# Making the second half of the first expert block's input during the last attention unit

## The chip, the cores and the metric

The kernel runs on one core of a Trainium2 chip. The metric is device time in microseconds (us), of one launch. PE is TensorE (matmuls), DVE is VectorE, ACT is ScalarE, POOL is GpSimd, and SP is SyncE, which here only issues DMA transfers.

## The reference

Attention with a learned relative-position bias, for 4 batches, 8 heads, 576 positions and head dimension 64, in float32; then a feed-forward layer over the 2304 tokens, with d_model 512 and d_ff 2048:

```
scores = q @ k.T / 8 + bias[h, i, j]
attn   = exp(scores - max) / (sum + 1e-9)
x      = (attn @ v), heads side by side        # 2304 x 512
h      = x @ w_in                              # 2304 x 2048
g      = h if h >= 1, 0 if h <= -1, else (h + 1)^2 / 4
out    = g @ w_out                             # 2304 x 512
```

All matmuls reach float32 accuracy by splitting an operand into a high part (rounded to the type that PE multiplies) and a low part (what rounding took away), and adding two or three products.

## The kernel before

**Three stages.** First the bias table is made (up to about 100 us, line 186 on). Then come 16 attention units, one for each pair of heads `p` and batch `b`, numbered `n = 4 p + b` (line 644). Each has five steps `k`: `scores` (line 493) multiplies queries and keys, DVE adds the bias and takes the maximum, ACT does the exponential; `transposes`, `shared` and `split` (lines 563, 581, 545) turn the result and split it into high and low parts; `values` (line 603) multiplies by the values, once for each half of the positions, and writes the product transposed to the DRAM buffers `xT`. `recips` (line 591) writes the reciprocal row sums to `rT`. A unit's transposes and values lag behind its scores, so the last unit's `values` end well after its scores. Last comes the feed-forward stage (line 713): three blocks of 768 tokens, each in two halves `j` of 384 tokens. For each of 16 slices `f` of d_ff and each half, `up_proj` (line 725) does 12 matmuls of 384 columns, `act` (line 735) makes g and its two parts, and `down_proj` (line 746) does 9 matmuls of 512 columns, some half-slices later (`finish`, line 766).

**The input x.** `split_x` (line 431) makes one quarter of a half: head pair `k` (128 rows of d_model) by 384 tokens. It loads two products from `xT` and the reciprocals from `rT`, broadcast over 64 partitions. DMAs are issued by SP: two for `xT`, and two for each piece into which the reciprocals fall (one piece for the first half of block 0, three for its second half, which crosses two batches). Then it adds the two products (line 457 or 460), multiplies (458 or 461), casts to the high part on ACT (462), and subtracts for the low part (464 or 466). With `early` the three others run on POOL, without it on DVE.

**Where block 0's x is made.** The table `xt` gives, for the four quarters of the first half, the unit and step at which the load and the arithmetic are written (lines 698 to 702): units 14 and 15, all through one raw tile in `m_raw`. The second half is written at the start of the feed-forward stage (line 781 on), on DVE, with three raw tiles in turn (`ring`, lines 99 and 723), two of them in `m_raw2`, which lies where the attention's bias tiles were. Its high and low parts lie in `m_x1`, also in room that the attention gives back.

**Weights.** `weight` (line 105) loads the raw float64 weights, and ACT (lines 114, 115, 118), DVE (116) and POOL (119) turn them into a high and a low part. Slices 0 and 1 are made in unit 15 (`wt`), through one raw tile; slice f + 2 is written behind `up_proj` of slice f, with raw tiles in `m_raw` and `m_raw2`.

**The order of work.** Each engine takes its instructions in a fixed order, and an instruction that waits holds those behind it. That order is set when the program is built, by a planner that takes instructions by their place in the program text and by its own estimate of when their operands and tiles are free; it may move work ahead or back within these limits. Instructions passed to `pool` keep their written order up to unit 14 (`go`). SP's DMAs are one such order, too.

**Rooms.** A tile with a tag lies in one of the tag's buffers and waits until the tile that had it is done. Units 14 and 15 are the last to use the key tiles (`kh`, `kl`), the value tiles (`vs`) and the raw tiles (`qk`, `v`).

Of the kernel before, what the change touches and what calls it, by code (L numbers as in the profile page):

```python
# [8 lines left out]
F32 = mybir.dt.float32  # L9
F32R = mybir.dt.float32r  # L10
# [3 lines left out]
ALU = mybir.AluOpType  # L14
# [16 lines left out]
CB = sum(CBW)  # L31
CFG = dict(ex=(9, 2, 0, 2, 9), bb=5, mv=1, hi='pvvpv', rb='a', lag=(1, 1), dr=(3, 1, 2, 2, 2), pool=((0, 1), (2, 0), (2, 1), (3, 0), (3, 1)), sb=4, keep=1, drain=2, diag='a', rb2='v', eps='v', rc=2, rbb=1, hb=2, rawb=(2, 2), t=(3, 10, 7, 10, 16, 11, 12, 18), eb=4, seq=0, yl=(2, 4, 12, 15, 16, 18, 20, 22, 24, 28, 30), yr=(3, 8, 19, 23, 35), ns=(1,) * NG, fw=2, pb=(6, 9, 12, 14, 16), pq=22, tb=6, ub=12, w1=('p', 'p', 'p', 'p'), wcp=('v', 'a', 'a', 'v'), wl=('p', 'v', 'p', 'p'), ms='ppvp', low0='ppp', anch=(8, 8, 16, 23, 23), low1='ppp', ob=6, gb=3, fin=2, xt=((14, 0), (14, 1), (14, 2), (14, 4), (14, 4), (15, 0), (15, 1), (15, 3)), wt=((15, 1), (15, 4)), lastp=15, ch=(0, 24, 52, 84, 112, 144), sbf=('v', 'v', 'v', 'v', 'v'), bsE=(), ytail='p')
EPS = 1e-9
RB = 2
LASTP = CFG["lastp"]
XT = CFG["xt"]
# [12 lines left out]
@with_exitstack  # L49
def attn_cpb_moe_kernel(ctx, tc, qk, vL, cb, win, wout, lw, dd, ident, ii, out):  # L50
    nc = tc.nc
# [6 lines left out]
    TH = TB // 2  # L58
# [40 lines left out]
    ring = [(rps[0], 1)]  # L99

    def x_pool():
        turn[1] += 1
        return ring[turn[1] % len(ring)]
# [30 lines left out]
    def pool(ins):  # L134
        if KEEP and go[0]:
            tc.keep_in_program_order(ins)
# [49 lines left out]
    with ExitStack() as ph:  # L186
# [24 lines left out]
        diag = [ac.tile([P, P], F32, name=f"diag{i}") for i in range(2)]  # L211
# [6 lines left out]
        pq = cp.tile([P, 2, C, H], F32, name="pq")  # L218
# [176 lines left out]
        for G in range(NG):  # L395
# [6 lines left out]
            i, g = G // 5 + 1, G % 5  # L402
# [28 lines left out]
    def split_x(blk, k, j, early=False):  # L431

        src = xT[k][blk // TB][:, :, TH * j : TH * j + TH].rearrange("(s d) i c -> d s i c", s=2)
        rp, n_ = x_pool()
        r = rp.tile([P, 3, TH], F32, tag="x", name=f"x{blk}_{k}_{j}", bufs=n_)
        for i in range(2):
            nc.sync.dma_start(out=r[D * i : D * i + D, 0:2], in_=src[:, :, i])
        c0 = blk + TH * j
        c1 = c0
        while c1 < c0 + TH:  # L440
            t = c1 % S
            e = min(c0 + TH, c1 - t + (512 if t < 512 else S))
            for i in range(2):
                at = 512 * i + t if t < 512 else 1024 + D * i + t - 512
                row = rT[k][c1 // S][at : at + e - c1].unsqueeze(0)
                nc.sync.dma_start(out=r[D * i : D * i + D, 2, c1 - c0 : e - c0], in_=row.to_broadcast((D, e - c1)))  # L446
            c1 = e

        z = (2 * (blk // TB) + j) % 3
        h = xps[z].tile([P, TH], F32R, tag=f"xh{k}", name=f"xh{blk}_{k}_{j}")  # L450
        l = xps[z].tile([P, TH], F32R, tag=f"xl{k}", name=f"xl{blk}_{k}_{j}")
        xs[blk, k, j] = h, l
        x = r[:, 0]

        def parts():
            if early:
                early[0](nc.gpsimd.tensor_tensor(out=x, in0=x, in1=r[:, 1], op=ALU.add))
                early[0](nc.gpsimd.tensor_tensor(out=x, in0=x, in1=r[:, 2], op=ALU.mult))
            else:
                nc.vector.tensor_tensor(out=x, in0=x, in1=r[:, 1], op=ALU.add)  # L460
                nc.vector.tensor_tensor(out=x, in0=x, in1=r[:, 2], op=ALU.mult)
            nc.scalar.copy(h, x)
            if early:
                early[0](nc.gpsimd.tensor_tensor(out=l, in0=x, in1=h.bitcast(F32), op=ALU.subtract))  # L464
            else:
                nc.vector.tensor_tensor(out=l, in0=x, in1=h.bitcast(F32), op=ALU.subtract)  # L466

        if early:
            return parts
        parts()  # L470

    with ExitStack() as ph:
# [154 lines left out]
        xlo = {}  # L627

        def drain(keep, mid=None, at=0):
            while len(queue) > keep:  # L630
# [6 lines left out]
        def step(i_):  # L637
            for m in range(3):
                for t, i in STEPS:
                    if t == 20 - 10 * m + i_ and 0 < n + m < N:  # L640
                        preps[n + m][i]()

        go[0] = True
        for n in range(N):
            p, b = n // B, n % B
            if n + 2 < N:
                preps[n + 2] = prep(n + 2)
            es[n] = []
            if n >= LASTP:
                go[0] = False  # L650
            for k in range(5):
                e, later = scores(n, k, qkv[n], bias[p])
                es[n].append(e)
                exps = [False]

                def exp_():
                    if not exps[0]:
                        exps[0] = True
                        for f in later:
                            exps.append(f())  # L660

                if CFG["ex"][k] == 0:
                    exp_()
                step(2 * k)
                if b == B - 1 and p + 1 < NP:
                    bias.setdefault(p + 1, []).append(load_bias(p + 1, k))

                def tr(n=n, k=k):
                    half = k // 2 if k < 4 else 1
                    if k in (0, 2):  # L670
                        w = 256 + D * half
                        eT[n, half] = (
                            (tp0, tp1)[half].tile([P, 9, w], F32R, tag=f"hi{half}", name=f"hi{n}_{half}"),
                            (tp0, tp1)[half].tile([P, 9, w], F32R, tag=f"lo{half}", name=f"lo{n}_{half}"),
                        )
                    transposes(n, k, es[n], eT[n, half])
                    if k in (1, 4):
                        shared(n, half, es[n], eT[n, half])

                def rc(n=n):  # L680
                    recips(n)

                if k in (1, 4):
                    def av(n=n, half=0 if k == 1 else 1):
                        values(n, half, es[n], eT[n, half], qkv[n]["v"])
                    queue.append([tr, rc] if k == 4 else [tr])
                    late.append([CFG["lag"][0 if k == 1 else 1], [av]])
# [25 lines left out]
    with ExitStack() as ph:  # L713
# [162 lines left out]
```

## Time and profile before

| what | value |
|---|---|
| median of 3 runs | 815.49 us (813.03 to 820.22) |
| profiled execution | 815.15 us, of which the span of the trace is 813.4 us |
| PE busy, share of the span | 90% |
| DVE, ACT, POOL busy | 61%, 57%, 51% |
| mean granted clock of PE | 0.96 |
| 40 slices of the span, PE busy in tenths, slices 18 to 22 | 9, 7, 5, 9, 9 |

The span is cut into 40 slices of 20.3 us. The chain of waits names, backwards from the end, what released each instruction. A wait of an engine is shown as the idle time ahead of an instruction and what ended it.

### The profile page before, as it was taken

Reading aid. Unit: us, or ns where it says so; the run is one execution under the profiler, and the core shown is the slowest. Engines: PE = TensorE matmul, PEld = TensorE weight load, DVE = VectorE, ACT = ScalarE, POOL = GpSimd, SP = SyncE. Lnnn points to the kernel's source line nnn. Section 1 sums busy time; section 2 is a strip of 40 time slices with the busy share of each in tenths; the row PEclk is TensorE's granted clock in tenths of the full one; section 3 lists DMA queues with packets and bytes.
Section 4 is the critical chain, followed back from the end, with each engine's and each line's share of the span. In section 5 each row is a group of like instructions: output and inputs, shape, how many; then the busy total and the mean of one; then the engine's idle time right before and its main releaser. Section 6 shows DMA issues by size and latency. Waiting matters only on the chain. (4 is left out here: it accounts for less than half of the span.)

```text
span 813.4 us, 13433 instructions
## 1 busy us (share of the span) xinstructions
PE 732.9 (90%) x4692; PEld 645.8 (79%) x4692; DVE 499.6 (61%) x1021; ACT 467.2 (57%) x1014; POOL 418.3 (51%) x385
## 2 busy tenths in 40 slices
PE   2766789899989999987599989999999999999998
PEld 1232579898989989986489888999999999999996
DVE  8999868788768888866475566276322243222222
ACT  1986668788878888877398854343222233222222
POOL 5774767788766878874177744222222222222221
PEclk9967999999999999998889999999999999999999
DMA  6667787876786687435566454054000012000002
GB/s 195 181 193 207 205 197 209 234 196 176 186 247 165 165 238 175 115 106 169 178 210 206 145 176 114 1 158 134 20 1 1 1 30 77 1 1 1 1 0 79
DMA packets 58660, 103.60 MB, mean 127 GB/s; under 512 B 12496, under 2 KB 32608, under 8 KB 58592
## 3 DMA queue, kind: packets, MB, share of 16 engines
q1 hardware_dynamic: 44976, 83.08, 35.5%
q0 software_dynamic: 2304, 9.96, 6.0%
q10 hardware_dynamic: 11312, 9.70, 3.9%
q8 instruction: 37, 0.61, 0.3%
q14 instruction: 31, 0.25, 0.1%
HBM read 67.63 MB, written 25.12 MB: 114 GB/s over the span
## 5 line engine op out<-in xcount | busy, mean ns | idle before, releaser
L743 POOL TENSOR_TENSOR gl<-c,gh 128x384 fp32r<-128x384 f32 x96 | 101.9, 1061 | 247.5 <-ACT gh L742 225.0
L740 ACT ACTIVATE c<-c,half_s 128x384 f32<-128x384 f32 x96 | 59.1, 615 | 169.0 <-DVE c L739 169.0
L730 PE MATMUL h<-xh,wi 128*128 128x384 f32 x384 | 132.6, 345 | 12.3 <-DVE c L741 6.4
L739 DVE TENSOR_SCALAR c<-h 128x384 f32<-128x384 f32 x96 | 53.3, 555 | 147.2 <-PE h L732 144.2
L731 PE MATMUL h<-xl,wi 128*128 128x384 f32 x384 | 131.4, 342 | 1.0 <-POOL xl L464 0.7
L732 PE MATMUL h<-xh,wi 128*128 128x384 f32 x384 | 131.4, 342 | 0.7 <-POOL wi L119 0.7
L557 POOL TENSOR_TENSOR lo<-c,hi 128x512 fp32r<-128x512 f32 x75 | 101.9, 1363 | 58.4 <-DVE hi L556 55.9
L753 PE MATMUL y<-wo,gl 128*128 128x512 f32 x288 | 114.2, 396 | 0.0
L752 PE MATMUL y<-wo,gh 128*128 128x512 f32 x288 | 113.9, 396 | 0.0
L751 PE MATMUL y<-wo,gh 128*128 128x512 f32 x288 | 112.6, 391 | 0.0
L510 DVE CUSTOM_DVE_ANT_0 e<-S,bias 128x576 f32<-128x576 f32 x128 | 93.8, 745 | 21.1 <-PE S L508 19.9
L517 ACT ACTIVATE e<-e,mx 128x576 f32<-128x576 f32 x128 | 99.7, 780 | 4.5 <-DMA v<-in_vL_dram 1.9
L507 PE MATMUL S<-kh,qa 128*128 128x288 f32 x256 | 79.5, 326 | 18.5 <-DMA kh<-kh 6.9
L730 PEld LDWEIGHTS h<-xh,wi 128*128 128x128 f32 x384 | 73.5, 191 | 20.8 <-DVE c L741 9.9
L741 DVE TENSOR_TENSOR c<-h,c 128x384 f32<-128x384 f32 x96 | 53.3, 556 | 50.3 <-ACT c L740 50.3
L742 ACT CAST gh<-c 128x384 fp32r<-128x384 f32 x96 | 49.2, 512 | 51.2 <-DVE c L741 50.1
L731 PEld LDWEIGHTS h<-xl,wi 128*128 128x128 f32 x384 | 73.5, 191 | 6.0 <-DVE xl L466 1.3
L572 PE MATMUL T<-id_s,e 128*128 128x128 f32 x512 | 74.1, 278 | 2.6 <-ACT e L517 1.5
L732 PEld LDWEIGHTS h<-xh,wi 128*128 128x128 f32 x384 | 73.5, 191 | 1.1 <-POOL wi L119 1.1
L508 PE MATMUL S<-ls,qa 128*128 128x288 f32 x256 | 72.3, 300 | 0.0
L507 PEld LDWEIGHTS S<-kh,qa 128*128 128x128 f32 x256 | 48.6, 190 | 26.4 <-DVE mx L510 11.8
L572 PEld LDWEIGHTS T<-id_s,e 128*128 128x128 f32 x512 | 61.6, 143 | 4.3 <-ACT e L517 1.9
(141 smaller groups left out, 1557.5 us busy)
## 6 DMA issues: line engine op xcount, KB each, us to landing
bias_d<-y SPq DMA_DIRECT2D x36, 295.5 KB, 3.3
qk<-in_qk_dram SPq DMA_DIRECT2D x16, 608.0 KB
qa<-in_qk_dram POOLq DMA_DIRECT2D x16, 608.0 KB, 6.6
x<-xT SPq DMA_DIRECT2D x48, 192.0 KB, 3.4
rawi<-in_win_dram SPq DMA_DIRECT2D x16, 512.0 KB, 4.6
rawo<-in_wout_dram SPq DMA_DIRECT2D x16, 512.0 KB, 3.7
v<-in_vL_dram SPq DMA_DIRECT2D x16, 320.0 KB, 3.4
qa<-ls SPq DMA_DIRECT2D x32, 152.0 KB, 3.4
```

Source lines behind the costliest of these rows:

```text
L507: nc.tensor.matmul(ps[:, hf, :HS], qs[:, qc], kh[:, kc : kc + HS], start=True, stop=False)
L510: nc.vector.tensor_tensor_reduce(out=ev.rearrange("p (a b) -> p a b", a=2), in0=ps[:, :, :HS], in1=bias[k][:, S * j : S * j + S].rearrange ...
L517: lambda ev=ev, j=j: nc.scalar.activation(ev, ev, AF.Exp, bias=mx[:, j : j + 1], scale=-1.0, accum_out=sm[:, 4 * j + k : 4 * j + k + 1])
L557: r = nc.gpsimd.tensor_tensor(out=lo, in0=m, in1=hi.bitcast(F32), op=ALU.subtract)
L572: nc.tensor.transpose(ps[:, tb, :], e[:, c0 : c0 + P], id_s)
L730: nc.tensor.matmul(ps[:, :TH], wh_, xh, start=k == 0, stop=False)
L731: nc.tensor.matmul(ps[:, :TH], wh_, xl, start=False, stop=False)
L732: nc.tensor.matmul(ps[:, :TH], wl_, xh, start=False, stop=k == NK - 1)
L743: nc.gpsimd.tensor_tensor(out=gl, in0=c, in1=gh.bitcast(F32), op=ALU.subtract)
L751: nc.tensor.matmul(y, gh[:, c], wo[f][0], start=f == 0, stop=False)
L752: nc.tensor.matmul(y, gh[:, c], wo[f][1], start=False, stop=False)
L753: nc.tensor.matmul(y, gl[:, c], wo[f][0], start=False, stop=f == NF - 1)
```

## The change

The table `xt` becomes `xa`: for each half `j` and each quarter, the step at which its load is written, the step of its arithmetic, the room of its raw data, and the engine (`p` POOL, `v` DVE). The second half of block 0 is now written in unit 15, two quarters on POOL and two on DVE. Three of its raw quarters lie in a buffer of the tags `kh`, `kl` and `vs`, the fourth in the one raw tile in `m_raw`. The last quarter of the first half moves to a buffer of the bias tag and is written some steps earlier. The high and low parts of the second half lie in the attention's raw tiles: three to a `qk` buffer, one to a `v` buffer (`x_tile`); `a_load` stays open to the end for that, and `m_x1` goes. In the later blocks the three raw tiles of x are one of `m_raw`, one of `m_x2` (which had two), and the room of the raw weights in `m_raw`. The arithmetic on x, the number of DMAs and their sizes stay as they are.

```
-CFG = dict(... xt=((14, 0), (14, 1), (14, 2), (14, 4), (14, 4), (15, 0), (15, 1), (15, 3)) ...)
+CFG = dict(xa=((((14, 0), (14, 1), '', 'p'), ((14, 2), (14, 4), '', 'p'),
+                ((14, 4), (15, 0), '', 'p'), ((14, 3), (15, 1), 'bias', 'p')),
+               (((15, 0), (15, 1), 'kh', 'p'), ((15, 0), (15, 2), 'kl', 'v'),
+                ((15, 1), (15, 3), 'vs', 'p'), ((15, 1), (15, 4), '', 'v'))) ...)
...
+    lp = ctx.enter_context(tc.tile_pool(name="a_load", side="right", bufs=2))
     bp = loads.enter_context(tc.tile_pool(name="a_bias", side="right", bufs=CFG["bb"]))
-    lp = loads.enter_context(tc.tile_pool(name="a_load", side="right", bufs=2))
...
+    def x_tile(z, k, part, name):
+        if z != 1:
+            return xps[z].tile([P, TH], F32R, tag=f"x{'hl'[part]}{k}", name=name)
+        at = 2 * k + part
+        g = min(at // 3, 2) + (at == 7)
+        if at % 3 == 0 or at == 7:
+            tag, w, n_ = ("qk", QW, CFG["rawb"][0]) if g < 2 else ("v", 10 * D, CFG["rawb"][1])
+            room[g] = lp.tile([P, w], F32R, tag=tag, name=name, bufs=n_)
+        c0 = TH * (at % 3 if at < 6 else 0)
+        return room[g][:, c0 : c0 + TH]
...
-            if early:
-                early[0](nc.gpsimd.tensor_tensor(out=x, in0=x, in1=r[:, 1], op=ALU.add))
-                early[0](nc.gpsimd.tensor_tensor(out=x, in0=x, in1=r[:, 2], op=ALU.mult))
+            if early == "p":
+                pool(nc.gpsimd.tensor_tensor(out=x, in0=x, in1=r[:, 1], op=ALU.add))
+                pool(nc.gpsimd.tensor_tensor(out=x, in0=x, in1=rr, op=ALU.mult))
             else:
                 nc.vector.tensor_tensor(out=x, in0=x, in1=r[:, 1], op=ALU.add)
...
-                    if (n, k) == XT[2 * i]:
-                        xlo[i] = split_x(0, i, 0, [pool])
-                    if (n, k) == XT[2 * i + 1]:
-                        xlo[i]()
+                    for j in range(2):
+                        ask, make, home, e = XA[j][i]
+                        if (n, k) == ask:
+                            r = None
+                            if home:
+                                po, w, n_ = dict(kh=(qp, QW, CFG["hb"]), kl=(qp, QW, 2), vs=(qp, 10 * P, 2), bias=(bp, 2 * S, CFG["bb"]))[home]
+                                r = po.tile([P, w], F32, tag=home, name=f"rx{j}_{i}", bufs=n_)
+                                r = r[:, : 3 * TH].rearrange("p (a b) -> p a b", a=3)
+                            xe[i, j] = split_x(0, i, j, e, r)
+                        if (n, k) == make:
+                            xe[i, j]()
...
-        xps.append(ph.enter_context(tc.tile_pool(name="m_x1", bufs=1)))
+        xps.append(None)
...
-            ring[1:] = [(xp, 2)] * 2
+            ring[1:] = [(xp, 1), (rps[0], 0)]
```

## Rows read from the trace of the kernel before

**Rows 1.** Busy time by stretch: length, PE, PEld, DVE, ACT, POOL (instructions), granted clock, DMA, GB/s.
```profile
370.00:388.60 18.60, 15.77 (x78) 13.77 (x77) 11.27 (x18) 13.69 (x33) 7.57 (x6) 0.74 0.67 194
388.60:413.00 24.40, 14.51 (x51) 11.28 (x51) 12.29 (x19) 12.15 (x22) 7.60 (x6) 0.78 0.62 190
413.00:470.00 57.00, 54.59 (x271) 48.28 (x270) 35.44 (x49) 48.37 (x88) 42.94 (x33) 1.00 0.56 181
```

**Rows 2.** Waits of PE from 412 us to the end: total, times, longest.
```profile
PE h L730 <- DVE c L741: 2.6, 2, 2.4
```

**Rows 3.** PE in order of time: start, length, line, [idle before, what ended it].
```profile
388.59 0.52 PE L730 MATMUL h<-xh,wi 128*128 128x384 f32 x1
...
391.12 0.44 PE L730 MATMUL h<-xh,wi 128*128 128x384 f32 x1 [1.57 <-DVE c L741]
...
403.81 0.69 PE L730 MATMUL h<-xh,wi 128*128 128x384 f32 x1 [3.95 <-ACT xh L462]
...
408.71 0.52 PE L730 MATMUL h<-xh,wi 128*128 128x384 f32 x1
...
412.98 0.38 PE L730 MATMUL h<-xh,wi 128*128 128x384 f32 x1
...
416.44 0.34 PE L730 MATMUL h<-xh,wi 128*128 128x384 f32 x1
...
418.55 0.39 PE L751 MATMUL y<-wo,gh 128*128 128x512 f32 x1
...
420.63 0.33 PE L730 MATMUL h<-xh,wi 128*128 128x384 f32 x1
```

**Rows 4.** SP's DMA issues in order of time: start, length, line, count.
```profile
395.48 1.25 SPq L437 DMA_DIRECT2D x<-xT  x2
396.77 3.80 SPq L446 DMA_DIRECT2D x<-rT  x6
400.62 0.58 SPq L109 DMA_DIRECT2D rawi<-in_win_dram  x1
```

**Rows 5.** PE instructions from 388.5 to 412.9 us, lines 730, 751, 752.
```profile
388.50:412.90 24.40, 6.30 (x13) 0.78 0.62 190
388.50:412.90 24.40, 1.81 (x4) 0.78 0.62 190
388.50:412.90 24.40, 1.18 (x3) 0.78 0.62 190
```

**Rows 6.** DVE in order of time around the attention's end.
```profile
388.83 0.56 DVE L739 TENSOR_SCALAR c<-h 128x384 f32<-128x384 f32 x1 [1.29 <-PE O L614]
...
390.50 0.56 DVE L741 TENSOR_TENSOR c<-h,c 128x384 f32<-128x384 f32 x1 [1.11 <-ACT c L740]
```

**Rows 7.** PE, then POOL, in order of time: what frees the rooms.
```profile
348.12 0.29 PE L529 MATMUL S_L<-ls,qa 128*128 128x288 f32 x1
...
365.12 0.31 PE L614 MATMUL O<-lo,vs 128*128 128x320 f32 x1
...
367.25 1.02 POOL L464 TENSOR_TENSOR xl<-x,xh 128x384 fp32r<-128x384 f32 x1 [0.62 <-ACT xh L462]
```

**Rows 8.** ACT's group of casts to x's high part, 340 to 410 us: busy, mean ns, idle before.
```profile
L462 ACT CAST xh<-x 128x384 fp32r<-128x384 f32 x8 | 4.1, 510 | 14.2 <-DVE x L461 9.2 <-POOL x L458 5.1
```

**Rows 9.** POOL, then DVE, in order of time: x's arithmetic side by side and alone.
```profile
378.04 1.12 POOL L464 TENSOR_TENSOR xl<-x,xh 128x384 fp32r<-128x384 f32 x1 [2.68 <-ACT xh L462]
...
378.22 1.35 DVE L460 TENSOR_TENSOR x<-x 128x384 f32<-128x384 f32 x1
...
395.18 0.55 DVE L460 TENSOR_TENSOR x<-x 128x384 f32<-128x384 f32 x1
```

**Rows 10.** POOL in order of time: the last step of slice 2's first weight.
```profile
407.88 1.28 POOL L119 TENSOR_TENSOR wi<-ai,wi 128x512 fp32r<-128x512 f32 x1 [13.04 <-ACT wi L118]
```

**Rows 11.** The page's DMA issues: count, KB each, median us to landing.
```profile
x<-xT SPq DMA_DIRECT2D x48, 192.0 KB, 3.4
```

**Rows 12.** POOL in order of time: the last step of slice 15's second weight.
```profile
498.99 1.62 POOL L119 TENSOR_TENSOR wo<-ao,wo 128x512 fp32r<-128x512 f32 x1
```

More of the change, by code (lines that the diff above doesn't have):

```diff
@@ L31 @@
 CB = sum(CBW)
-CFG = dict(ex=(9, 2, 0, 2, 9), bb=5, mv=1, hi='pvvpv', rb='a', lag=(1, 1), dr=(3, 1, 2, 2, 2), pool=((0, 1), (2, 0), (2, 1), (3, 0), (3, 1)), sb=4, keep=1, drain=2, diag='a', rb2='v', eps='v', rc=2, rbb=1, hb=2, rawb=(2, 2), t=(3, 10, 7, 10, 16, 11, 12, 18), eb=4, seq=0, yl=(2, 4, 12, 15, 16, 18, 20, 22, 24, 28, 30), yr=(3, 8, 19, 23, 35), ns=(1,) * NG, fw=2, pb=(6, 9, 12, 14, 16), pq=22, tb=6, ub=12, w1=('p', 'p', 'p', 'p'), wcp=('v', 'a', 'a', 'v'), wl=('p', 'v', 'p', 'p'), ms='ppvp', low0='ppp', anch=(8, 8, 16, 23, 23), low1='ppp', ob=6, gb=3, fin=2, xt=((14, 0), (14, 1), (14, 2), (14, 4), (14, 4), (15, 0), (15, 1), (15, 3)), wt=((15, 1), (15, 4)), lastp=15, ch=(0, 24, 52, 84, 112, 144), sbf=('v', 'v', 'v', 'v', 'v'), bsE=(), ytail='p')
+CFG = dict(xa=((((14, 0), (14, 1), '', 'p'), ((14, 2), (14, 4), '', 'p'), ((14, 4), (15, 0), '', 'p'), ((14, 3), (15, 1), 'bias', 'p')), (((15, 0), (15, 1), 'kh', 'p'), ((15, 0), (15, 2), 'kl', 'v'), ((15, 1), (15, 3), 'vs', 'p'), ((15, 1), (15, 4), '', 'v'))), ex=(9, 2, 0, 2, 9), bb=5, mv=1, hi='pvvpv', rb='a', lag=(1, 1), dr=(3, 1, 2, 2, 2), pool=((0, 1), (2, 0), (2, 1), (3, 0), (3, 1)), sb=4, keep=1, drain=2, diag='a', rb2='v', eps='v', rc=2, rbb=1, hb=2, rawb=(2, 2), t=(3, 10, 7, 10, 16, 11, 12, 18), eb=4, seq=0, yl=(2, 4, 12, 15, 16, 18, 20, 22, 24, 28, 30), yr=(3, 8, 19, 23, 35), ns=(1,) * NG, fw=2, pb=(6, 9, 12, 14, 16), pq=22, tb=6, ub=12, w1=('p', 'p', 'p', 'p'), wcp=('v', 'a', 'a', 'v'), wl=('p', 'v', 'p', 'p'), ms='ppvp', low0='ppp', anch=(8, 8, 16, 23, 23), low1='ppp', ob=6, gb=3, fin=2, wt=((15, 1), (15, 4)), lastp=15, ch=(0, 24, 52, 84, 112, 144), sbf=('v', 'v', 'v', 'v', 'v'), bsE=(), ytail='p')
 EPS = 1e-9
@@ L35 @@
 LASTP = CFG["lastp"]
-XT = CFG["xt"]
+XA = CFG["xa"]
 NX = [((14, 0), (14, 1), (14, 1), (15, 0)), ((4, 0), (6, 0), (8, 0), (10, 0))]
@@ L429, in attn_cpb_moe_kernel, with split_x @@
     xs = {}
-    def split_x(blk, k, j, early=False):
-        src = xT[k][blk // TB][:, :, TH * j : TH * j + TH].rearrange("(s d) i c -> d s i c", s=2)
-        rp, n_ = x_pool()
-        r = rp.tile([P, 3, TH], F32, tag="x", name=f"x{blk}_{k}_{j}", bufs=n_)
+    room = {}
+    def x_tile(z, k, part, name):
[8 more added lines that the diff above has]
+        return room[g][:, c0 : c0 + TH]
+    def split_x(blk, k, j, early=False, raw=None):
+        src = xT[k][blk // TB][:, :, TH * j : TH * j + TH].rearrange("(s d) i c -> d s i c", s=2)
+        if raw is None:
+            rp, n_ = x_pool()
+            if n_:
+                r = rp.tile([P, 3, TH], F32, tag="x", name=f"x{blk}_{k}_{j}", bufs=n_)
+                r, rr = r[:, 0:2], r[:, 2]
+            else:
+                r = rp.tile([P, 2 * DM], F32, tag="raw", name=f"x{blk}_{k}_{j}")[:, : 2 * TH].rearrange("p (a b) -> p a b", a=2)
+                rr = rp.tile([P, DM], F32, tag="a", name=f"xr{blk}_{k}_{j}")[:, :TH]
+        else:
+            r, rr = raw[:, 0:2], raw[:, 2]
         for i in range(2):
-            nc.sync.dma_start(out=r[D * i : D * i + D, 0:2], in_=src[:, :, i])
+            nc.sync.dma_start(out=r[D * i : D * i + D], in_=src[:, :, i])
         c0 = blk + TH * j
@@ L445, in split_x @@
                 row = rT[k][c1 // S][at : at + e - c1].unsqueeze(0)
-                nc.sync.dma_start(out=r[D * i : D * i + D, 2, c1 - c0 : e - c0], in_=row.to_broadcast((D, e - c1)))
+                nc.sync.dma_start(out=rr[D * i : D * i + D, c1 - c0 : e - c0], in_=row.to_broadcast((D, e - c1)))
             c1 = e
         z = (2 * (blk // TB) + j) % 3
-        h = xps[z].tile([P, TH], F32R, tag=f"xh{k}", name=f"xh{blk}_{k}_{j}")
-        l = xps[z].tile([P, TH], F32R, tag=f"xl{k}", name=f"xl{blk}_{k}_{j}")
+        h = x_tile(z, k, 0, f"xh{blk}_{k}_{j}")
+        l = x_tile(z, k, 1, f"xl{blk}_{k}_{j}")
         xs[blk, k, j] = h, l
@@ L455, in parts @@
         def parts():
-            if early:
-                early[0](nc.gpsimd.tensor_tensor(out=x, in0=x, in1=r[:, 1], op=ALU.add))
-                early[0](nc.gpsimd.tensor_tensor(out=x, in0=x, in1=r[:, 2], op=ALU.mult))
+            if early == "p":
+                pool(nc.gpsimd.tensor_tensor(out=x, in0=x, in1=r[:, 1], op=ALU.add))
+                pool(nc.gpsimd.tensor_tensor(out=x, in0=x, in1=rr, op=ALU.mult))
             else:
                 nc.vector.tensor_tensor(out=x, in0=x, in1=r[:, 1], op=ALU.add)
-                nc.vector.tensor_tensor(out=x, in0=x, in1=r[:, 2], op=ALU.mult)
+                nc.vector.tensor_tensor(out=x, in0=x, in1=rr, op=ALU.mult)
             nc.scalar.copy(h, x)
-            if early:
-                early[0](nc.gpsimd.tensor_tensor(out=l, in0=x, in1=h.bitcast(F32), op=ALU.subtract))
+            if early == "p":
+                pool(nc.gpsimd.tensor_tensor(out=l, in0=x, in1=h.bitcast(F32), op=ALU.subtract))
             else:
@@ L626, in attn_cpb_moe_kernel @@
         queue, late = [], []
-        xlo = {}
+        xe = {}
         def drain(keep, mid=None, at=0):
```

## The prediction

> **What bounds the kernel now.** I began with the page's slices: PE is nearly full except where the attention hands over to the feed-forward stage. The busy times by stretch put numbers on it [rows 1]: from 413 us PE is busy at full clock, but in the 24.4 us from 388.6 it is busy for 14.5 us at a mean clock of 0.78. The list of PE's waits from 412 us to the end has 2.6 us in it [rows 2]; so whatever work PE has done by 413 us fixes the end, and time won before that point is won at the end.
>
> PE's order of time shows the handover [rows 3]. At 388.59 the attention's last value matmuls are over and the first matmul of slice 0's second half (up 0,1) begins. Then PE waits: for the activation of (0,0), and again and again for the high part of a second-half quarter, up to 3.95 us at once. After that wait it runs at half clock (1.2 GHz, by the mean of 0.78): a matmul of line 730 takes 0.52 us at 408.71 where one at 416.44 takes 0.34. Behind the missing x stands SP [rows 4]: one second-half quarter takes 1.25 + 3.80 = 5.05 us of issuing (8 DMAs), about the distance at which the quarters arrive, and slice 2's first weight is issued only behind the last of them, at 400.62.
>
> **What the hole costs.** From 388.59 to 412.98 is 24.39 us [rows 3]. In it PE does 13 matmuls of line 730, as many of 731 and 732 (39 of 384 columns), and 4 + 3 + 3 = 10 of 512 columns (751 to 753; the last has as many as 752) [rows 5]. At the full rate, pipelined, twelve 384s take 418.55 - 416.44 = 2.11 us (0.176 each) and nine 512s 420.63 - 418.55 = 2.08 (0.231 each) [rows 3]. So 39 x 0.176 + 10 x 0.231 = 9.2 us of work took 24.4.
>
> **What the change removes.** With the second half ready before the attention ends, the 12 matmuls of (0,1) lie before 388.6. What stays is the activation of (0,0): it waits for the attention's last matmul, and its second half ends at 390.50 + 0.56 [rows 6], after which PE restarts at 391.12 as it does now. From there 27 x 0.176 + 10 x 0.231 = 7.1 us reach the point of 412.98, at 398.2. The gain before costs is 412.98 - 398.2 = **14.8 us**. A lower clock at the restart would cost 0.52 - 0.34 = 0.18 us a matmul, 2.2 us for a dozen; today PE restarts at 391.12 with 0.44, a first matmul at full clock, after the same value matmuls, so I take 0.
>
> **Is x ready in time?** The rooms decide. The key tiles are free when unit 14's scores are done, at 348.4; the value tile after 365.12 + 0.31, and the shared raw tile after 367.25 + 1.02 = 368.27 [rows 7]. SP needs 4 x 5.05 = 20.2 us for the 32 DMAs that move. Two quarters fit before 365.4; the third takes to 370.5, the fourth to 375.5, landing 3.4 us later [rows 11], and the chain add, multiply, cast, subtract of 4 x 0.55 ends near 381. That is 7 us before 388.6. The raw loads of slices 0 and 1 on the same queue move back by up to 5 us; slice 1's first weight then still comes about when PE restarts, so 0, with that cover thin.
>
> **What it adds.** *ScalarE.* Four casts of 0.51 us [rows 8]; one of them lies before 388.6 today, so 3 x 0.51 = 1.5 us more. ACT is busy 13.7 of 18.6 us there [rows 1] and its exponentials, casts and copies feed the last transposes, so I charge all of it: **+1.5**. *Waits in front of them.* ACT has three waits for POOL's multiply, 5.1 us together [rows 8], 1.7 each, and behind such a cast stand the attention's own casts. Two new quarters are on POOL: 2 x 1.7 = **+3.4**. For the two on DVE the bounds are 0 and 1.7 each (the row's 9.2 us for DVE all lies behind 388.6); I take 0, since the nearest one, the DVE quarter already made before 388.6, has no wait. *POOL*: 6 operations of about 1.0 us [rows 9] in 11 us of idle time [rows 1], 0. *VectorE*: 6 operations of 0.55 us come, but about as many that stand before 388.6 today go to POOL, 0. *TensorE*: 9 more matmuls before 388.6, 1.6 us at full rate, against 18.60 - 15.77 = 2.8 us of idle time [rows 1]: 0, at most 2.9 at half clock.
>
> *Weights.* Slice 2's first weight takes from 400.62 to 409.16, 8.5 us [rows 4, 10], and is wanted when PE has done (1,0), (1,1) and ten of the 512s, about 7 us after its restart. It must be issued near 389. Its raw room lies over the bias tiles, free before that, and SP is idle by then, so 0. *Later blocks.* The third raw tile becomes the weights' own, free when slice 15 is done, about 500.6 us [rows 12]. At 412.98 PE begins on slice 2, and a slice takes 2 x (2.11 + 2.08) = 8.4 us, so slice 15 comes 13 x 8.4 later, at 522, or 512 with the gain, and block 1 one slice behind: over 15 us for two quarters through that room, so 0. The single wait of 2.4 us in [rows 2] may go or move: 2.4 either way.
>
> **Sum.** 14.8 - 1.5 - 3.4 = 9.9 us less. The profiled execution took 815.15 us (0.34 below the median of 815.49): 815.15 - 9.9 = **805.2 us**.
>
> **A rule that speaks against it.** A DVE add of 0.55 us took 1.35 while POOL's subtract ran from 378.04 to 379.16 [rows 9]. The change puts x on both engines at once. The Trainium skill, SBUF — State Buffer, section "Who interferes with whom", says that a DVE instruction with two SBUF inputs contends with a GpSimd instruction that reads SBUF, and that the loser fully blocks; by that rule the trace agrees, for the DVE add ends just after POOL's operation.
>
> **Rivals.**
> (a) *Both engines block each other.* Six DVE operations at 0.80 us more each are 4.8 us, in front of the attention's evictions in DVE's order: 805.2 + 4.8 = 810.0. For it: the 1.35. Against: DVE has 18.60 - 11.27 = 7.3 us idle there [rows 1], and its attention work reads PSUM. Chance 0.10. This is the case of the rule above.
> (b) *Weights take the place of x.* If slice 2's weight still ended at 409.16, its matmuls would come not near 412 but at 409.2, and eight more 512s (1.8 us) would be done ahead: about 5 us won, 810. For it: one raw tile, ACT busy 48.4 of 57 us after 413 [rows 1]. Against: SP's queue is what held it. Chance 0.12.
> (c) *The second half comes no earlier in effect*: the planner leaves its loads behind others, and the hole stays: 813 to 817, taken as 815. For it: SP must fit 20 us more of issuing into unit 15. Chance 0.10.
> (d) *Slower: the attention's end is held up.* ACT takes its order strictly; if each of the four casts stands in front of attention work and waits as casts do behind 388.6 today (9.2 us in three waits, 3.1 each, and up to 5.05 where SP paces them), then 4 x 5.05 = 20.2, less the 14.8 won and plus 1.5 for the casts: 815.15 + 6.9 = 822. It is slower once the mean wait passes (14.8 - 1.5) / 4 = 3.3 us. Against: the rooms above open early enough. Chance 0.08.
>
> **The numbers.** My forecast has 0.60, with 800.4 (the gain of 14.8 in full) to about 809 as its own range: DVE's casts waiting as POOL's do cost 3.4 more. The range over all takes in (a) and (b) and reaches to 813, where the costs together (1.5 + 6.8 + 4.8) leave 1.7 us: that leaves out (d), most of (c), and a little below. About 1% (8 us, below 807.3 or above 823.6 by the median) is what a measurement here can tell from no change. Faster by over 1%: 0.60, nearly all of the forecast and little else. Slower by over 1%: the worse part of (d), 0.07. Same: the rest, 0.33.
>
> **What would show it.** After the change, the 12 matmuls of (0,1) should stand before the attention's last value matmul, and PE's waits for the high part of x should be gone behind it. The attention's end should move from 388.6 to about 393 (1.5 + 3.4), with waits of ACT's cast for POOL in front; if it moves by over 13, (d) holds. A wait of line 732 for POOL's line 119 behind it, or of line 730 for ACT's line 118, is (b). DVE's x operations at over 1 us are (a). SP issuing second-half quarters behind 388 is (c), and would make the prediction wrong; so would a new PE wait near 500 to 530, where the raw tile of the weights is shared.

## The result

The changed kernel took 807.56 us (median of 4 runs, 805.41 to 808.29), the kernel before 815.12 beside it (4 runs, 813.03 to 820.22): a ratio of 0.9894, 95% interval [0.9844, 0.9944]. Run once more with more runs it had 0.9865 [0.9832, 0.9897]. The forecast was 805.2 us, 0.988 of the median before. So the kernel became about 1% faster, as forecast. The terms of the sum came out differently, though, and the mechanism is told below.

**Busy time by stretch after** (columns as in [rows 1]; the profiled execution took 806.87 us, its span is 805.1):

```profile
370.00:391.00 21.00, 17.78 (x114) 16.37 (x113) 11.86 (x25) 14.64 (x36) 9.17 (x9) 0.92 0.53 150
391.00:405.00 14.00, 8.98 (x25) 6.07 (x26) 8.20 (x11) 11.81 (x22) 7.50 (x6) 0.76 0.83 273
405.00:470.00 65.00, 63.06 (x320) 56.91 (x319) 39.24 (x61) 52.67 (x96) 47.51 (x37) 1.00 0.60 187
```

The hole is still there, shorter: 14 us with 9 us of busy PE at a mean clock of 0.76, where [rows 1] had 24.4 us with 14.5. ACT is now the busy engine in it: 11.8 of 14 us, where before it had 12.2 of 24.4.

**PE after, in order of time:** first the matmul that transposes the sums of unit 13, which serves as a landmark below, then the attention's end and the handover (compare [rows 3]).

```profile
340.96 0.27 PE L619 MATMUL R<-id_s,sum 128*9 128x128 f32 x1
...
387.47 0.75 PE L633 MATMUL O<-hi,vs 128*128 128x320 f32 x4
...
390.25 0.31 PE L635 MATMUL O<-lo,vs 128*128 128x320 f32 x1
392.26 0.44 PE L758 MATMUL h<-xh,wi 128*128 128x384 f32 x1 [1.70 <-ACT xh L483]
...
393.13 0.34 PE L760 MATMUL h<-xh,wi 128*128 128x384 f32 x1
396.10 0.79 PE L779 MATMUL y<-wo,gh 128*128 128x512 f32 x1 [2.64 <-ACT gh L770]
397.04 0.80 PE L780 MATMUL y<-wo,gh 128*128 128x512 f32 x1
398.01 0.80 PE L781 MATMUL y<-wo,gl 128*128 128x512 f32 x1 [0.17 <-POOL gl L771]
398.60 0.63 PE L779 MATMUL y<-wo,gh 128*128 128x512 f32 x1
...
400.31 0.63 PE L780 MATMUL y<-wo,gh 128*128 128x512 f32 x1
...
404.09 0.45 PE L760 MATMUL h<-xh,wi 128*128 128x384 f32 x1 [0.66 <-POOL wi L119]
```

Nine of the twelve matmuls of (0,1) stand before the attention's last value matmul at 390.25. The last quarter's three come behind it (lines 758 to 760 are 730 to 732 of before; 779 to 781 are 751 to 753). Then PE waits 2.64 us for the activation of (0,0), and the fourteen matmuls of 512 columns that follow take from 396.10 to 402.73, 6.6 us, where at full rate they take 14 x 0.231 = 3.2. Two things make up the 3.4 us. From 398.60 to 400.31 a matmul follows every 0.43 us, not every 0.23; with the mean granted clock of 0.76 from 391 to 405 us that is the lower level, 1.2 GHz, which came after two waits with only three matmuls between them. The first three, though, take 2.5 us, where three at 0.43 take 1.3: the second and the third wait for low parts that POOL has just finished, that of the weight (395.71 + 1.27) and that of the activation. So about 1.2 of the 3.4 us are waits for POOL, and about 2.2 are the clock.

```profile
395.71 1.27 POOL L119 TENSOR_TENSOR wo<-ao,wo 128x512 fp32r<-128x512 f32 x1 [8.75 <-ACT wo L118]
```

PE's order has changed as well. Before, the twelve matmuls of (1,0), from 391.12 on, stood ahead of the first down matmul, and covered the time until the activation of (0,0):

```profile
393.31 0.40 PE L751 MATMUL y<-wo,gh 128*128 128x512 f32 x1
```

Now the down matmuls stand first, and nothing covers it. The reason is in SP's list.

**SP after, in order of time** (compare [rows 4]): three second-half quarters; slice 0's second weight; slice 2's and 3's first; and among the last two slice 1's first.

```profile
368.74 1.25 SPq L458 DMA_DIRECT2D rx<-xT  x2
370.03 4.83 SPq L467 DMA_DIRECT2D rx<-rT  x6
374.96 1.25 SPq L458 DMA_DIRECT2D rx<-xT  x2
376.25 3.80 SPq L467 DMA_DIRECT2D rx<-rT  x6
380.15 1.25 SPq L458 DMA_DIRECT2D x<-xT  x2
381.44 5.58 SPq L467 DMA_DIRECT2D x<-rT  x6
387.12 0.53 SPq L109 DMA_DIRECT2D rawo<-in_wout_dram  x1
387.69 0.90 SPq L109 DMA_DIRECT2D rawi<-in_win_dram  x2
...
394.69 1.52 SPq L109 DMA_DIRECT2D rawi<-in_win_dram  x2
```

The last quarter's loads end at 387.02 and not near 375.5. Slice 0's second weight is issued behind them, at 387.12, and slice 1's first, which takes the same raw tile after it, at 394.69 or later, so that the matmuls of (1,0) can't go ahead. In the kernel before, these two loads were issued here:

```profile
370.98 0.59 SPq L109 DMA_DIRECT2D rawo<-in_wout_dram  x1
...
378.33 0.33 SPq L109 DMA_DIRECT2D rawi<-in_win_dram  x1
```

**ACT after, from the attention's last copy on** (start, length):

```profile
390.60 0.42 ACT L636 COPY x<-O 128x320 f32<-128x320 f32 x1 [0.89 <-PE O L635]
...
391.69 0.51 ACT L483 CAST xh<-x 128x384 fp32r<-128x384 f32 x1 [0.67 <-DVE c L767]
392.11 0.76 ACT L114 ACTIVATE rawo<-rawo,floor_s 128x512 int32<-128x512 uint16 x1
392.77 0.64 ACT L115 ACTIVATE ao<-rawo 128x512 f32<-128x512 f32 x1
393.32 0.60 ACT L768 ACTIVATE c<-c,half_s 128x384 f32<-128x384 f32 x1
393.82 0.76 ACT L114 ACTIVATE rawi<-rawi,floor_s 128x512 int32<-128x512 uint16 x1
394.47 0.65 ACT L115 ACTIVATE ai<-rawi 128x512 f32<-128x512 f32 x1
395.03 0.61 ACT L118 CAST wo<-ao 128x512 fp32r<-128x512 f32 x1
395.54 0.51 ACT L770 CAST gh<-c 128x384 fp32r<-128x384 f32 x1
```

This is the handover in one view. PE waits for line 770. On ACT the cast of x's last quarter and five steps of two weights (slice 0's second and slice 2's first) stand before it; lines 768 and 770, the activation itself, are 1.1 us of the 4.4 from 391.69.

**PE's waits after, from 388 us to the end** (compare [rows 2]), besides the 2.64, 1.70, 0.66 and 0.17 us above:

```profile
PE h L758 <- DVE c L769: 2.5, 3, 1.1
```

**A landmark for comparing.** The start of a profiled execution differs by up to 6 us between executions, so times are counted from unit 13's transposing matmul (338.48 before, 340.96 after); in all kernels below it comes 16.7 or 16.8 us behind that of unit 12. Three lengths follow: from it to the end of the attention's last value matmul; from there until PE has done 30 us of feed-forward matmuls, at the prediction's 0.176 and 0.231 a piece; and the rest of the span.

| kernel | attention's end | handover | both | rest |
|---|---|---|---|---|
| before | 50.3 | 43.0 | 93.3 | 381.6 |
| changed | 49.6 | 35.6 | 85.2 | 378.9 |
| changed, again | 49.6 | 35.6 | 85.2 | 378.7 |
| weights ahead of x | 57.7 | 30.9 | 88.6 | 378.3 |
| one slice ahead | 52.4 | 32.3 | 84.7 | 379.9 |
| casts off ScalarE | 49.1 | 37.8 | 86.9 | 377.8 |
| both of these (all weights ahead) | 52.9 | 31.6 | 84.5 | 381.4 |
| second half all on POOL | 49.3 | 35.5 | 84.8 | 380.7 |
| no reciprocal loads | 54.4 | 36.3 | 90.7 | 378.6 |
| second half for nothing | 51.0 | 28.1 | 79.1 | 378.4 |
| before, ring alone | 50.8 | 42.8 | 93.6 | 382.4 |
| before, no reciprocal loads | 51.2 | 38.1 | 89.3 | 380.0 |

The change won 8.1 us up to that point, and 2.7 in the rest. Each row is one profiled execution; the two of the changed kernel agree within 0.2 us.

### The profile page after: what moved, and what is told of

Same layout as the page of the kernel before. It is cut to its first block, busy times and chain, and to the rows that moved or that the text cites. A ratio compares the mean times of both kernels' runs of the same rounds, so it can differ in the third digit from the quotient of the medians.

```text
span 805.1 us, 13437 instructions
## 1 busy us (share of the span) xinstructions
PE 728.2 (90%) x4692; PEld 645.3 (80%) x4692; DVE 486.2 (60%) x1015; ACT 466.5 (58%) x1014; POOL 422.3 (52%) x391
## 5 line engine op out<-in xcount | busy, mean ns | idle before, releaser
L758 PE MATMUL h<-xh,wi 128*128 128x384 f32 x352 | 120.1, 341 | 5.2 <-DVE c L769 2.5
L760 PE MATMUL h<-xh,wi 128*128 128x384 f32 x352 | 119.2, 339 | 1.1 <-POOL wi L119 1.1
L759 PE MATMUL h<-xl,wi 128*128 128x384 f32 x352 | 119.1, 338 | 0.1
L769 DVE TENSOR_TENSOR c<-h,c 128x384 f32<-128x384 f32 x96 | 53.4, 556 | 50.3 <-ACT c L768 50.0
L770 ACT CAST gh<-c 128x384 fp32r<-128x384 f32 x96 | 49.1, 512 | 58.8 <-DVE c L769 58.0
L758 PEld LDWEIGHTS h<-xh,wi 128*128 128x128 f32 x352 | 66.4, 189 | 11.7 <-DVE c L769 4.7
L528 PEld LDWEIGHTS S<-kh,qa 128*128 128x128 f32 x256 | 49.6, 194 | 27.5 <-DVE mx L531 12.3
L759 PEld LDWEIGHTS h<-xl,wi 128*128 128x128 f32 x352 | 66.3, 188 | 3.1 <-DVE xl L487 0.4
L760 PEld LDWEIGHTS h<-xh,wi 128*128 128x128 f32 x352 | 66.2, 188 | 1.7 <-POOL wi L119 1.7
```

The source lines that it names most:

```text
L528: nc.tensor.matmul(ps[:, hf, :HS], qs[:, qc], kh[:, kc : kc + HS], start=True, stop=False)
L758: nc.tensor.matmul(ps[:, :TH], wh_, xh, start=k == 0, stop=False)
L759: nc.tensor.matmul(ps[:, :TH], wh_, xl, start=False, stop=False)
L760: nc.tensor.matmul(ps[:, :TH], wl_, xh, start=False, stop=k == NK - 1)
```

## The experiments

Line numbers in the rows are those of each kernel's own text. The first expectations name three theories: A, ScalarE's backlog bounds the handover; W, the weights of slices 0 and 1 come too late; X, the last quarter of x does, because of SP's queue.

**The changed kernel again.**

> The changed kernel once more, on the chip of the other runs of this call, so that they can be set against it and not only against the kernel before. Both theories expect what was measured, a ratio of 0.989 (0.984 to 0.994) to the kernel before, and the same order of events: SP issues x from 364 to 387 us without a pause, the second raw weight of slice 0 is issued at 387 and the first of slice 1 behind it, and PE waits behind the attention's end until about 404.

800.55 us, 0.9865 [0.9832, 0.9897]; both lengths as in the first profile.

**Weights ahead of x.** The steps of slices 0 and 1 are written ahead of the second half's, and one and three key groups earlier.

```
-wt=((15, 1), (15, 4))
+wt=((15, 0), (15, 1))
...
+                for f in range(2):
+                    if (n, k) == WT[f]:
+                        with tc.issue_after(last_e.ins):
+                            weights(f)
                 for i in range(NK):
                     for j in range(2):
...
-                for f in range(2):
-                    if (n, k) == WT[f]:
...
```

> The changed kernel with the raw loads of slices 0 and 1 written ahead of the loads of x, at steps 0 and 1 of the last unit and not 1 and 4; nothing else. Theory W (the handover now waits for the weights of slices 0 and 1, because their four loads stand on SP behind 32 loads of x): these weights are ready before the attention ends, PE's waits of 2.6 us for the activation's cast and of 0.7 us for the low part of slice 1's weight go, and it is 3 to 5 us faster than the changed kernel, 803 to 805. Rival X (the handover waits for the last quarter of x): that quarter is issued 1.3 to 2.5 us later, so it is 1 to 3 us slower, 808 to 811. Rival A (ScalarE, busy 19.3 of 22 us behind the attention's end, is the bound): the weights' ScalarE work only moves in front of the attention's last casts and delays them by as much; within 1 us of the changed kernel.

803.94 us, 0.9907 [0.9875, 0.994], some 3 us slower than the changed kernel beside it, though the two intervals overlap. The handover is tight, 30.9 us, but the attention ends 8 us later. PE's waits from 380 to 405 us:

```profile
PE T_s L609 <- ACT diag L560: 2.3, 1, 2.3
PE h L758 <- ACT xh L483: 1.5, 1, 1.5
...
```

(1,0) stands ahead of the down matmuls again, and the waits for the activation and for weights are gone: W names the handover's waits rightly. But the attention's own matmuls wait instead, so earlier weights are no cure: their work costs more in front of the end than behind it.

**One DMA where two loaded a piece of reciprocals**, alone and with the weights ahead.

```
-            for i in range(2):
-                at = 512 * i + t if t < 512 else 1024 + D * i + t - 512
-                row = rT[k][c1 // S][at : at + e - c1].unsqueeze(0)
-                nc.sync.dma_start(out=rr[D * i : D * i + D, ...], in_=row.to_broadcast((D, e - c1)))
+            row = rT[k][c1 // S][...].rearrange("(i t) -> i t", i=2)[...]
+            nc.sync.dma_start(out=rr[:, ...], in_=row.unsqueeze(1).to_broadcast((2, D, w)))
```

> The changed kernel with one DMA in place of two for each piece of the reciprocals (a source pattern that covers both heads), so a second-half quarter takes 5 DMAs and not 8, and 15 of the 48 issues of block 0's x go. Order of writing as in the changed kernel. Theory W: at 0.6 us each the raw weights are issued some 8 us earlier, near 379, and it is 3 to 5 us faster than the changed kernel, 803 to 805. Rival X: the last quarter comes 8 us earlier, also 3 to 5 us faster, since its wait of 1.7 us and what follows go. Rival A: within 1 us of the changed kernel.

> Both edits: raw loads of slices 0 and 1 written ahead of x, and one DMA for each piece of the reciprocals. Theory W: weights ready as in the first, x ready as in the second: the best of the four, 5 to 7 us faster than the changed kernel, 801 to 803, with PE restarting about 2.5 us behind the attention's end and no wait after. Rival X: as the second alone or 1 us slower. Rival A: within 1 us of the changed kernel.

848.74 us, 1.0452 [1.0416, 1.0488], and 854.25, 1.0518 [1.0483, 1.0552]. The count of issues fell but not their time, and the reciprocals came late all through the feed-forward stage. SP around the second half, alone; then two of the waits of the whole span:

```profile
374.84 5.25 SPq L466 DMA_DIRECT2D rx<-rT  x3
...
382.31 4.71 SPq L466 DMA_DIRECT2D x<-rT  x3
```

```profile
DVE x L481 <- DMA x<-rT: 38.5, 10, 5.5
...
PE h L757 <- DVE c L768: 30.0, 11, 5.7
```

Three issues took 4.71 us and more where six of the pairs took 3.80 to 5.58. Why, is not shown. So this says nothing on the theories; the edit replaced one cost by a larger one.

**Casts off ScalarE.** The first block's eight quarters are cast on the engine of their arithmetic.

```
-            nc.scalar.copy(h, x)
+            if early == "p":
+                pool(nc.gpsimd.tensor_copy(h, x))
+            elif early:
+                nc.vector.tensor_copy(h, x)
+            else:
+                nc.scalar.copy(h, x)
```

> The changed kernel with one thing different: the high parts of the first block's early x quarters are cast on the engine that does the quarter's arithmetic (POOL or DVE) instead of on ACT. Theory A (ScalarE's backlog bounds the handover: ACT was busy 19.3 of 22 us from 391 to 413 us in the changed kernel, and the last cast of x and the activation of the first slice queue in it): the casts' 8 x 0.51 us leave ACT and its order has no wait for POOL's multiply any more (7.6 us of such waits from 345 to 391 us); the second-half quarters are ready earlier, and the kernel is 3 to 5 us faster than the changed one: ratio to the kernel before about 0.981. Theory W/X (SP's queue bounds it: the x loads are issued without a pause from 364.7 to 387.0 us and the weights behind them): the last quarter's data and the weights come when they came, and the time is that of the changed kernel within 1 us, about 0.987.

805.31 us, 0.9919 [0.9888, 0.995]: no faster, rather slower. PE's waits in it from 380 to 405 us, and one from 338 to 387 us:

```profile
PE y L784 <- ACT wo L118: 2.5, 1, 2.5
PE h L763 <- DVE xh L486: 1.2, 1, 1.2
...
PE O L638 <- POOL hi L580: 4.2, 1, 4.2
```

With the casts gone from ACT, the wait of 2.6 us for the activation became one of 2.5 us for the weight itself, and the attention waited 4.2 us for POOL. A falls as the single cause.

**Both.**

> Both edits: slice 0's and 1's weights are loaded and split ahead of the second half of x, and the casts of the early x quarters are off ACT. The weights ahead alone were 0.4% slower than the changed kernel, with the attention's end 8 us later, since ACT did the weights' casts in front of the attention's. Theory A: with the x casts gone from ACT, 4 us of its work and its waits for POOL are out of the attention's tail: 3 to 5 us faster than the weights ahead alone, ratio about 0.985 to 0.987, and PE's half-clock stretch behind the attention shrinks. Theory W/X: x then comes last in SP's queue, so the wait for the last quarter stays, ratio about 0.990 as the weights ahead alone.

805.06 us, 0.9921 [0.989, 0.9952], not the 0.985 to 0.987 of A. The two lengths are 84.5 us together, against 85.2: what the handover won, the attention lost.

**The ring alone**, in the kernel before, with the lines of `split_x` that this needs and the ring's turn set to where it stands in the changed kernel.

```
...
-            ring[1:] = [(xp, 2)] * 2
+            ring[1:] = [(xp, 1), (rps[0], 0)]
+            turn[1] = 4
```

> The kernel before with only the change to the rooms behind the attention: the third raw tile belongs to the weights and the first two x quarters of block 1 go through a raw room of the weights; the second half of the first block's x is made as before. It tells where about 2.7 us of the changed kernel's gain came from that arose only behind the handover (the kernel before had one PE wait of 2.4 us at 469.9 us and a clock of 0.88 in 466 to 480 us; the changed kernel has 1.00 there). If the ring did that: 2 to 3 us faster than before, ratio about 0.997. If it came from the earlier second half: no difference, 1.000.

814.04 us, 1.0015 [0.9993, 1.0038]: it does nothing. PE's waits from 409 us to the end:

```profile
PE h L735 <- DVE c L746: 3.6, 3, 2.6
```

The long wait of [rows 2] is still there, so it is not the ring that makes the changed kernel's rest shorter. With the second half made early the rest lies between 377.8 and 381.4 in the table, and by what steps it gets shorter is open.

**Second half all on POOL.**

```
-((15, 0), (15, 2), 'kl', 'v') ... ((15, 1), (15, 4), '', 'v')
+((15, 0), (15, 2), 'kl', 'p') ... ((15, 1), (15, 4), '', 'p')
```

> The changed kernel with one thing different: the two second-half quarters that VectorE makes are made on POOL, as the others are. Where x on both engines at once makes them block each other (rival a of the prediction), or where DVE's x operations stand in front of the attention's evictions, this is faster than the changed kernel, by up to 3 us (0.983). Where neither matters, POOL's chain becomes the longer one: four quarters of add, multiply and subtract at about 1.0 us each are 12 us on POOL behind loads that end at 387 us, two quarters each end 1.5 us later, and the time is 1 to 3 us above the changed kernel's (0.989).

805.25 us, 0.9911 [0.9881, 0.9941], the same as the changed kernel within what the intervals tell; 84.8 against 85.2 us by the landmarks. Half on VectorE is worth nothing here, and costs nothing.

**No reciprocal loads.** Changed kernel:

```
-        while c1 < c0 + TH:
+        while c1 < c0 + TH and not (blk == 0 and j):
...
+        if blk == 0 and j:
+            rr = r[:, 1]
```

> The changed kernel, where the four second-half quarters of the first block are multiplied by their own second raw plane instead of by the reciprocals (that part of the computation is changed), and so the 24 DMAs that load the reciprocals of these quarters are left out: 8 DMAs a quarter become 2, 3.8 us of SP's issuing less for each, 15 us in all. Everything else has the same operations. Theory A as the first expectations put it (ScalarE is the bound) has already lost: without the casts of x on ACT the handover was no shorter. Theory Q (SP's queue is the bound): the quarters' data are there by about 377 us and the first weights are issued some 10 us earlier; PE's wait for the first slice's activation (2.6 us), the half-clock stretch behind it and the wait for the third matmul's weights (0.7 us) go; 4 to 5 us faster than the changed kernel, ratio to the kernel before about 0.982. Theory T (the attention's tail is full: whatever preparation of weights is moved in front of its end holds that end up by as much): the attention's end comes 3 to 5 us later as measured from the unit before last, the handover is that much shorter, and the time is that of the changed kernel within 1.5 us, about 0.987 to 0.990.

806.79 us, 0.9907 [0.9881, 0.9933]. SP had 15 us less to issue, and nothing was won, so Q falls as the single cause. PE in order of time:

```profile
394.90 0.44 PE L760 MATMUL h<-xh,wi 128*128 128x384 f32 x1 [2.87 <-DVE c L771]
...
406.39 0.69 PE L760 MATMUL h<-xh,wi 128*128 128x384 f32 x1 [2.94 <-DVE c L771]
```

(1,0) is ahead of the down matmuls, and no wait for x or a weight is left behind the attention; what remains are two waits for activations, the second new, and a low clock behind each (a mean of 0.57 from 395 to 399 us and of 0.56 from 405 to 410). The weights' work moved ahead and the attention ended 4.8 us later (54.4 against 49.6), as T has it, but the handover was not shorter for it.

**One slice ahead:** the weights' loop stands ahead of x's, as in the weights ahead, with `wt` unchanged.

> The changed kernel with the steps of slice 0's and 1's weights ahead of the second half's steps at the same key group instead of behind them; no weight's step is moved to another key group. On SP the second weight of slice 0 goes ahead of the last two second-half quarters, one load ahead of sixteen. Theory Q: the down matmuls' wait behind the attention (2.6 us for the activation that stands behind this weight's operations on ACT) goes: 2 to 3 us faster than the changed kernel, about 0.984. Theory T: that weight's ACT, DVE and POOL work (0.76 + 0.64 + 0.61 us on ACT) moves in front of the attention's end and holds it up: same within 1.5 us, 0.987 to 0.990.

803.63 us, 0.9862 [0.9833, 0.989]: as the changed kernel. The attention ended 2.8 us later and the handover was 3.3 us shorter, T's trade again.

**The kernel before without the reciprocal loads**, the same edit.

> The kernel before, where the four second-half quarters of the first block are multiplied by their own second raw plane instead of by the reciprocals (that part of the computation is changed), and so the 24 DMAs that load these reciprocals are left out. It tests the prediction's reading that SP's issuing, 5.05 us a quarter, paces the second half in the kernel before. If so, the quarters follow at 1.25 us of issuing, and what then paces them is DVE's and ACT's work of about 2.2 us a quarter: the hole of 24.4 us shrinks by 3 x 2.8 = 8 us or more, ratio about 0.988, that is as much as the whole change gives. If rooms or ACT pace them, it shrinks by 3 us or less: 0.996 or above.

809.31 us, 0.9932 [0.9905, 0.9958], 4.0 us by the landmarks, between the two expectations. SP's issuing of the reciprocals was about half of what the whole change gives, and not all that paced the second half.

**The second half for nothing.**

```
     def split_x(blk, k, j, early=False, raw=None):
+        if blk == 0 and j:
+            xs[blk, k, j] = xs[blk, k, 0]
+            return lambda: None
...
```

> The changed kernel where the second half of the first block's columns takes the x tiles of the first half (that part of the computation is changed): the 32 DMAs, 12 operations on POOL and DVE and 4 casts on ACT of the second half's four quarters are gone altogether, and the matmuls of the second half have their x with the first half's. It bounds what any way of making this x earlier or elsewhere could still give. Prediction's sum: with x for nothing the attention's end would be where it was and PE would restart at the activation of the first slice, the full 14.8 us ahead of the kernel before: 800, ratio about 0.982, some 5 us (0.6%) ahead of the changed kernel. Theory T (the rest of the handover is the preparation of weights and activations, which ACT must do either in front of the attention's end or behind it): the time is within 2 us of the changed kernel, 0.986 to 0.990, with PE waits for activations (c, L772) and for wi or wo of slices 0 to 3 in place of those for x, and half clock behind them.

797.61 us, 0.9817 [0.9795, 0.9839]: the prediction's number for x without costs, 0.982, and not T's. By the landmarks it is 93.3 - 79.1 = 14.2 us ahead of the kernel before; the prediction had 14.8. Set against the changed kernel by the ratios the gain is less sure: the intervals, to 0.9839 here and from 0.9832 for the changed kernel run again, overlap by a little. PE, its only wait of the handover, and then the busy times of the ten microseconds from the attention's end:

```profile
388.47 0.44 PE L761 MATMUL h<-xh,wi 128*128 128x384 f32 x1 [2.18 <-DVE c L772]
```

```profile
386.00:396.00 10.00, 7.82 (x42) 7.16 (x42) 6.47 (x11) 9.11 (x17) 6.12 (x6) 1.00 0.47 168
```

The clock stays at 2.4 GHz through the handover (1.00), after a wait of 2.18 us and no second one. The changed kernel had 9 us of busy PE in 14, at 0.76.

Of the kernels that make all of x, none beat the changed kernel by more than the intervals; one slice ahead equals it.

## Why the prediction was right

**The size of the hole** was right: 14.8 us, and with the second half for nothing the handover is 43.0 - 28.1 = 14.9 us shorter (14.2 with the attention's end, which comes 0.7 later there).

**The costs of 4.9 us** (1.5 for the casts, 3.4 for ACT's waits) are near what x's work did cost over both lengths, 85.2 - 79.1 = 6.1 us, so that 14.2 - 6.1 = 8.1 us were won here, against 9.9. That is luck, for the cost arose in another place and from other causes. The prediction put it on the attention's end, from 388.6 to about 393. That end did not move: 50.3 us behind the landmark before, 49.6 after. And the term of 3.4 hardly came. ACT's waits for POOL's multiply in front of the attention's end are 6.2 us, against 5.1 in [rows 8]:

```profile
ACT xh L483 <- POOL x L479: 5.5, 2, 3.6
...
ACT xh L483 <- POOL rx L479: 0.7, 1, 0.7
```

The first line is of quarters of the first half: the raw data of the two new quarters on POOL lie in tiles named `rx`. So these two cost 0.7 us of waits, not 2 x 1.7.

What x's work cost lies behind the attention's end: the changed kernel has 35.6 us of handover and the second half for nothing 28.1. Of these 7.5, 2.64 and 0.66 us are waits, 6.6 - 3.2 = 3.4 what the fourteen matmuls took too long (POOL's low parts and the clock), and 3 x 0.176 = 0.5 late matmuls of (0,1): 7.2 together. The first wait, of 1.70, has its like there, of 2.18.

Two things that the prediction did not have can account for the attention's end staying where it was. The work of slice 0's second weight and of slice 1's first, which in the kernel before stood in front of it, had gone behind it: with weights ahead the end comes 2.8 to 8.1 us later. And PE's clock was higher. The attention's last 20 value matmuls began 46.5 us behind the landmark (at 387.47), where before they began 43.9 behind it, but they took 3.1 us and not 6.5: the last one 0.31 us, and before 0.47.

```profile
382.34 1.41 PE L612 MATMUL O<-hi,vs 128*128 128x320 f32 x4 [0.48 <-DVE lo L548]
...
388.33 0.47 PE L614 MATMUL O<-lo,vs 128*128 128x320 f32 x1
```

With the second half for nothing they begin late as well, at 46.3, so it is not the second half's work that delays them. The matmuls of (0,1) in front of them may: nine here and twelve there, 1.6 and 2.1 us at full rate, which the prediction put at 0. (In the weights ahead the value matmuls took 5.7 us, which is 2.6 of its 8.1.) What the clock and the weights' place are each worth was not measured by itself.

**The step that failed** is "Is x ready in time?". It had the raw loads of slices 0 and 1 move back by up to 5 us, at no cost. Slice 0's second weight went from 370.98 to 387.12, 13.7 us by the landmarks. Its decoding came to stand between the attention's last copy and the first activation, and slice 1's first weight, behind it in the one raw tile, came too late for (1,0) to cover that activation: the wait of 2.64 and that of 0.66 us. It also had x ready near 381, with two quarters issued before 365.4. But SP takes its DMAs in order: a load of the first half stood 3.8 us, to 364.67, until POOL's subtract had freed the one raw tile, and the second half's loads stood behind it. Only six of the 32 DMAs were out by then.

```profile
SPq L458 <- POOL xl L485: 3.8, 1, 3.8
```

So the last quarter's loads ended at 387.02 and its multiply at 389.73, and its cast came at 391.69, behind the attention's last copies in ACT's order:

```profile
389.17 0.56 DVE L482 TENSOR_TENSOR x<-x 128x384 f32<-128x384 f32 x1 [0.56 <-DVE lo L569]
```

**The restart at full clock** ("so I take 0") held for the first matmuls, 0.44 us at 392.26 as today, and failed behind them. The second wait, which the prediction did not foresee, was followed by half clock, and that cost about the 2.2 us that it had named as the price of a lower clock.

**The rest of the span** brought 2.7 us more. The prediction had "2.4 either way" for the one wait in [rows 2]; but PE's waits there are as long as before, 2.5 us in three pieces against 2.6. About 1.7 of the 2.7 is the clock: from 470 to 480 us its mean is 0.83 before and 1.00 after. So the total of 805.2 against the profiled 806.87 is near, by luck too, because 1.8 us too much at the handover and the 2.7 uncounted nearly cancel, and the rest lies within the differences at the start (2.5 us later here).

**Rivals.** (a) VectorE's operations for x took, with one exception, their plain time:

```profile
374.27 1.00 DVE L481 TENSOR_TENSOR rx<-rx 128x384 f32<-128x384 f32 x1
...
387.33 0.55 DVE L481 TENSOR_TENSOR x<-x 128x384 f32<-128x384 f32 x1
```

That is 0.45 us and not 4.8, and all on POOL is no faster. (b) fell in its form: slice 2's first weight was even ready ahead of slice 1's. But weights did take x's place, those of slices 0 and 1. (c) holds in effect for one quarter of four, though its sign, second-half issues behind 388 us, did not show: they ended at 387.02. (d) fell: the end did not move. Of the new wait feared near 500 to 530 us, where the weights' raw tile is shared, 0.5 us is there (0.2 before).

**What stays open** is which part of x's work costs the 6.1 us. Less ScalarE work, less issuing, and less VectorE work, each alone, won nothing; all of it together won 6.1. The weights' steps were never left out, so what they cost behind the attention is read from PE's and ACT's order and from the trade in the table, not measured by itself. The planner may also make a new order for each of these kernels, so that an edit can change more than the one thing it names.

## What to carry to other kernels

When work is pulled ahead into a stage that is busy on several in-order queues, count what it pushes back on each of them, and look for it behind the stage's end: there it stands in front of the first instruction that the next stage waits for. Price the whole gain with the work left out altogether, here 14.2 us of which the change won 8.1; reordering, in the kernels tried here, at most moved cost between the two sides. Compare profiles from a landmark that all versions share, or the start's own differences (6 us here) hide what a 1% change did.

## What the runs showed of the hardware

One transfer that broadcasts two rows to 64 partitions each, with the two rows outermost in its pattern, was not cheaper than two transfers of one row each: three such issues took 4.71 and 5.25 us, the data came up to 5.5 us after DVE was ready for them, and the kernel took 4.5% longer [1.0416, 1.0488]. Other patterns were not tried.

PE's clock stayed at full after one wait of 2.18 us (second half for nothing), and was at half after waits of 1.70 and 2.64 us with three matmuls between them (the changed kernel), and after one of 2.87 us (no reciprocal loads). What decides between them is not shown here.
